# A transformer block on one core: the same 2931 operations in another written-out sequence

## The chip, the cores and the metric

The kernel runs on one core of one Trainium2 chip. The metric is the device time of one execution in microseconds. A core has five engines, each with a queue of its own that it works through in order: TensorE (PE, with the weight loads shown apart as PEld), VectorE (DVE), ScalarE (ACT), GpSimd (POOL) and SyncE (SP). SyncE issues the transfers (DMA) of this kernel. Engines wait for each other by semaphores.

## The reference

One transformer block on x of 2048 rows and 640 columns, in float32:

```python
x = A_x
h = x + _A_ref(_layernorm(x), A_wqkv, A_wo)      # attention
h2 = h + _B_ref(_layernorm(h), w_gate, w_up, w_down)

# _A_ref: 32 heads of 20; row s sees the 8 rows s, s-2, ..., s-14 that exist
logits = einsum("bhsd,bhswd->bhsw", q, kg) * 20 ** -0.5
attn = softmax(where(mask, logits, -1e9))
o = einsum("bhsw,bhswd->bhsd", attn, vg)          # then (o as rows) @ wo

# _B_ref, with 1728 hidden columns
(silu(x @ w_gate) * (x @ w_up)) @ w_down
```

Layernorm has no scale or shift; eps is 1e-5.

## The kernel before, in words

The 2048 rows are taken as four blocks of 512. Every product is done in three passes: each operand is split into a high part (a rounding copy on ScalarE, to fp32r) and a low part (a subtraction on VectorE), and TensorE adds high x high, low x high and high x low. So an operand that is made new costs one instruction on ScalarE and one on VectorE before the matmuls can start, and the matmuls are 512, 384 or 320 columns wide.

The stages, which overlap:

- Start: rows of x come in, are normed, transposed on TensorE (L627) and split (copy L629, subtraction L630). Then the q, k and v projections (L671), four column groups for each block. Results leave PSUM by ScalarE (L680 and others) and go to scratch in DRAM (L701 is a store of k or v rows).
- Attention: for each of 16 pairs of block and group, SyncE loads q (L724) and k and v windows (L728) back. VectorE multiplies q with k (L738, 2560 elements a partition), sums (L745), does the parts of the softmax (L756, L757, L767 to L769), multiplies with v (L773) and adds halves (L780, with 1280 or 640 elements). GpSimd adds some halves (L799). Stores of the attention's output are L813 and L816.
- Output projection: loads L919, splits L923 (ScalarE) and L924 (VectorE), matmuls L943 of 320 columns (L942 in the profile). Layernorm of h follows, with transposes L521, copies L523 and subtractions L513 and L524.
- FFN of blocks 0 and 1: 14 tiles of 128 hidden columns. A tile's weights are loaded (L993; or L999 where the split weights are read back from a store in DRAM), split (copies L994, L995; subtractions L1011), then come three gate passes into PSUM bank 5 and three up passes into bank 6 (five matmuls each, L1017), SiLU (L1040, ScalarE), the multiply by bank 6 (L1041, VectorE), the split of the result (L1051, L1052) and the down product (L1028), which is cut in five pieces of three matmuls into banks 0 to 4. The next tile's up passes need bank 6 back, so they wait for L1041.
- FFN of blocks 2 and 3 together: some tiles as above (L1123; for the last, narrow one L1044 to L1047), then the rest as paired products with fewer multiplications (L1101), whose sums are added on VectorE (L1278) out of banks 5 to 7 and whose operand combinations are made by L1259, L1260 and L1262. Last the down products (L1353, with L1344 and L1345 for their operands) and the final sums and stores (L1164, L1169, L1383).

What sets the order of the work: every operation is handed to `Plan.add` with its engine and what it reads and writes; it gets the next number (0 to 2930) and a set of operations it must come after. `Plan.order` then emits all operations by the tuple `ORDER`, holding an operation back only while one that it depends on is not out:

```python
place = {n: i for i, n in enumerate(ORDER)}
heap, out = [(place.get(n, n), n) for n in range(len(left)) if not left[n]], []
...
    n = heapq.heappop(heap)[1]
    out.append(n)
```

`ORDER` already satisfies the dependences, so it is emitted as it stands, and each engine's queue is the subsequence of its operations. The costs and priorities that `add` is given play no part. An operation is often several instructions (a pass of five matmuls, a piece of downs of three). Operation numbers that the steps below use, in the profiled execution of before: 59, 64, 67 transposes of the start (67 at 16.56 us); 143 to 147, 162 to 164 single matmuls of the first projection; 220 a store of v rows (L701), 264 the load of normed rows (L537), 519 and 521 a q and a k load; 268, 270, 272, 274 low parts of block 1's columns (L546) and 523 the attention product L738 at 56.01; 1396 to 1417, 1590 to 1610, 1710 to 1730 and 1768 to 1788 passes L1017 in the FFN (up passes 1417, 1608, 1728 and 1788 at 364.80, 411.06, 481.45 and 516.53); 848 the shorter L780, 1579 a low part L1052, 1495 an L1429 addition, 1592 the multiply L1041 at 410.33; 1555 a wo product; 868 the v load at 451.83, 1700 the weight load L993 at 450.82, 1664 the L999 load at 449.15, 1505, 1508 and 1511 loads L919, 1635 to 1639 the pieces of downs that end the use of 1664's slot; 1857 to 1860 pieces of downs of two matmuls, 1930 to 1932 products L1101 near 566.

Of the kernel before, what the change touches and what calls it, by code (L numbers as in the profile page):

```python
# [37 lines left out]
    10, 0, 2, 9, 36, 6, 11, 47, 1, 7, 3, 13, 12, 14, 18, 17, 8, 37, 38, 41, 39, 42, 133, 19, 44, 45, 134, 15, 43,  # L38
    135, 136, 16, 48, 21, 52, 22, 46, 40, 26, 49, 20, 23, 137, 138, 53, 54, 139, 25, 27, 140, 141, 24, 30, 50, 51,
    29, 31, 32, 142, 34, 62, 150, 151, 152, 153, 154, 155, 156, 157, 158, 159, 28, 83, 160, 161, 162, 163, 164, 72,  # L40
    33, 55, 79, 78, 82, 86, 64, 80, 87, 81, 94, 90, 65, 59, 60, 70, 66, 71, 67, 68, 69, 91, 63, 95, 143, 103, 102,
    144, 73, 145, 74, 98, 99, 106, 107, 184, 146, 248, 84, 56, 85, 76, 57, 61, 58, 88, 89, 147, 92, 111, 93, 96, 185,
    186, 187, 188, 189, 190, 165, 35, 97, 4, 149, 121, 114, 191, 75, 115, 192, 193, 166, 194, 195, 77, 196, 100, 197,
    198, 101, 104, 108, 105, 167, 168, 169, 170, 148, 5, 199, 171, 172, 173, 174, 118, 175, 176, 177, 178, 179, 180,
    181, 182, 202, 183, 203, 109, 249, 251, 130, 124, 253, 255, 259, 204, 116, 205, 208, 200, 122, 110, 117, 127,
    112, 214, 215, 509, 131, 206, 210, 113, 507, 209, 511, 254, 128, 119, 129, 512, 508, 211, 213, 125, 221, 212,
    230, 120, 252, 201, 216, 513, 222, 263, 207, 224, 250, 262, 123, 260, 232, 223, 256, 226, 257, 261, 219, 218,
    227, 126, 264, 521, 269, 519, 265, 132, 239, 225, 514, 515, 271, 516, 267, 270, 258, 229, 517, 273, 231, 237,
    220, 240, 266, 523, 275, 228, 518, 510, 238, 241, 242, 522, 268, 274, 272, 217, 276, 278, 279, 233, 243, 236,
    1012, 327, 235, 244, 324, 280, 525, 318, 282, 234, 321, 524, 247, 334, 323, 551, 320, 326, 283, 526, 527, 528,  # L50
    529, 520, 325, 530, 531, 246, 245, 322, 340, 553, 328, 286, 343, 281, 289, 290, 287, 319, 532, 533, 288, 337,
    331, 277, 284, 534, 535, 546, 547, 555, 548, 336, 329, 350, 291, 549, 550, 536, 556, 557, 344, 540, 1003, 294,
    335, 541, 552, 538, 342, 558, 539, 559, 545, 298, 330, 300, 345, 353, 296, 292, 560, 301, 332, 537, 333, 339,
    561, 285, 562, 544, 341, 542, 338, 302, 359, 355, 297, 356, 554, 351, 360, 293, 299, 361, 543, 352, 354, 349,
    295, 347, 377, 368, 357, 370, 348, 303, 305, 358, 307, 369, 583, 383, 372, 309, 371, 386, 563, 363, 585, 346,
    1015, 385, 564, 565, 566, 584, 567, 578, 573, 576, 577, 568, 569, 579, 570, 572, 580, 571, 313, 581, 587, 582,
    589, 590, 588, 591, 592, 593, 594, 575, 595, 596, 574, 597, 306, 310, 315, 304, 1006, 379, 314, 364, 308, 317,
    316, 373, 366, 365, 367, 376, 393, 362, 375, 615, 384, 380, 378, 311, 598, 599, 610, 611, 374, 396, 398, 425,
    402, 397, 428, 430, 415, 617, 382, 381, 586, 388, 432, 1009, 395, 434, 399, 387, 312, 394, 390, 392, 391, 612,
    600, 601, 613, 614, 605, 608, 619, 621, 426, 620, 604, 431, 647, 409, 603, 389, 411, 400, 622, 1028, 401, 412,  # L60
    403, 618, 602, 418, 414, 413, 416, 433, 435, 407, 417, 616, 429, 623, 607, 410, 427, 404, 419, 406, 408, 436,
    437, 606, 609, 1035, 422, 439, 420, 421, 445, 442, 405, 441, 1016, 452, 444, 443, 1004, 624, 625, 626, 627, 628,
    630, 461, 446, 447, 631, 633, 634, 635, 636, 637, 642, 643, 644, 645, 646, 649, 651, 653, 652, 654, 1010, 629,
    655, 656, 657, 648, 1013, 632, 438, 455, 1019, 440, 458, 424, 454, 423, 456, 678, 468, 457, 1005, 658, 450, 448,
    453, 638, 639, 1017, 449, 641, 640, 460, 1014, 459, 650, 470, 472, 451, 463, 462, 1020, 659, 464, 469, 482, 1021,
    1007, 660, 661, 662, 1025, 1022, 1023, 467, 663, 1026, 1011, 474, 466, 1024, 1027, 1008, 1029, 1030, 680, 674,
    675, 664, 1031, 1032, 676, 679, 682, 465, 683, 1052, 677, 684, 475, 665, 668, 1033, 1053, 1158, 484, 1036, 1037,
    666, 473, 1038, 1054, 479, 471, 478, 1039, 667, 1034, 1040, 1041, 1042, 485, 1061, 685, 1055, 1058, 1059, 1069,
    709, 1056, 686, 669, 687, 688, 1060, 1062, 480, 1043, 1065, 1057, 1070, 1044, 1045, 488, 501, 477, 689, 1100,
    1160, 476, 483, 1063, 1066, 481, 671, 690, 1159, 673, 672, 670, 711, 1046, 1071, 1064, 1073, 1074, 1067, 1068,  # L70
    691, 1163, 1050, 1047, 692, 1072, 1075, 1048, 693, 694, 1162, 489, 1076, 1077, 705, 499, 500, 497, 495, 486,
    1078, 487, 1049, 1161, 681, 1079, 1080, 1051, 1089, 1176, 1085, 1094, 713, 492, 1097, 1098, 1087, 498, 714, 502,
    1099, 1083, 1084, 1095, 1091, 1081, 1092, 1177, 1086, 1166, 496, 1096, 493, 1082, 1169, 1199, 710, 1088, 1093,
    1090, 1167, 490, 1168, 1164, 706, 707, 695, 503, 1179, 505, 1165, 1170, 504, 1171, 708, 1172, 1184, 715, 506,
    494, 1018, 697, 1201, 698, 716, 1200, 1185, 717, 1180, 1186, 700, 702, 1173, 1187, 1188, 718, 1182, 699, 1178,
    701, 1189, 1204, 703, 1202, 1181, 1190, 1174, 1203, 1207, 1175, 1198, 1208, 696, 712, 1191, 1197, 1210, 719,
    1209, 1192, 1193, 704, 1222, 1211, 1212, 1245, 720, 721, 722, 740, 1223, 1195, 1194, 1217, 1225, 1183, 1213,
    1230, 1214, 1206, 1233, 1196, 1226, 1228, 1215, 1219, 1221, 723, 724, 1246, 1220, 1224, 1216, 1231, 1232, 1205,
    1234, 742, 1227, 1268, 741, 1235, 736, 737, 738, 1249, 1248, 1251, 725, 726, 730, 1218, 727, 1240, 1236, 739,
    746, 1253, 729, 1237, 1241, 1243, 1256, 1247, 747, 1269, 1250, 1254, 1255, 1229, 744, 1110, 745, 743, 1271, 1257,  # L80
    1272, 1291, 1258, 1259, 1276, 748, 1244, 1260, 772, 1279, 1292, 1261, 1274, 749, 1242, 1270, 1238, 750, 1273,
    1239, 728, 1277, 1278, 1314, 751, 752, 1280, 753, 757, 755, 1281, 1264, 1295, 754, 1262, 1294, 1252, 1263, 1282,
    1299, 1300, 756, 1301, 1283, 1302, 731, 735, 1315, 1266, 1297, 733, 734, 1287, 1267, 1303, 1290, 758, 759, 760,
    1318, 1304, 1284, 1265, 1288, 1285, 1305, 1322, 1101, 1311, 1317, 1104, 1306, 1105, 1307, 1107, 761, 732, 1106,
    762, 1108, 1102, 1293, 1323, 1109, 774, 1103, 1324, 1296, 1286, 767, 1111, 1325, 1112, 1326, 768, 776, 1289,
    1309, 1337, 1328, 765, 1338, 1327, 1113, 1316, 769, 1114, 1115, 763, 1117, 766, 764, 775, 777, 1124, 1130, 803,
    1313, 770, 1341, 1345, 771, 1118, 1125, 1319, 1320, 1329, 1312, 1119, 1310, 778, 779, 1120, 1121, 780, 1340, 781,
    1339, 1127, 1275, 1122, 1298, 1308, 1348, 1332, 1126, 1349, 1350, 782, 1133, 1128, 1129, 1330, 1131, 1321, 1342,
    1132, 1346, 1331, 1360, 783, 784, 785, 1134, 1135, 1136, 1123, 786, 1347, 1351, 773, 787, 788, 1383, 805, 1334,
    1137, 1138, 1140, 1361, 1343, 1333, 1356, 1364, 1335, 1363, 1336, 1366, 1352, 789, 1362, 1365, 1367, 1406, 1139,  # L90
    1384, 1368, 799, 800, 1357, 1141, 801, 1142, 1369, 1116, 1371, 1370, 1374, 1143, 802, 791, 807, 1387, 806, 1386,
    1372, 1373, 1144, 1391, 1392, 1393, 1353, 1354, 794, 795, 1375, 1394, 1407, 1145, 1359, 1358, 1381, 1146, 1147,
    808, 1410, 1395, 796, 1376, 793, 1355, 1378, 809, 1397, 834, 1389, 1414, 1409, 1412, 1415, 792, 797, 1148, 1344,
    1149, 1150, 1396, 1382, 1379, 810, 798, 811, 1447, 1385, 1151, 1377, 812, 1405, 813, 1388, 1152, 1401, 1153,
    1398, 790, 814, 1416, 1420, 1429, 1156, 1430, 1157, 804, 1154, 1155, 1417, 1418, 1419, 1380, 1408, 815, 836, 816,
# [1481 lines left out]
```

## Time and profile before

| | |
|---|---|
| median of 3 runs | 836.1 us (834.64 to 836.66) |
| profiled execution | 836.91 us, span 834.6 us |
| granted TensorE clock, mean | 1.0 |
| busy: PE / PEld / DVE / ACT / POOL | 823.7 / 709.1 / 744.3 / 434.9 / 26.3 us |
| DMA | 211.09 MB, mean 253 GB/s |

Busy times are those of the span. L12 is line 12 of the kernel before; the code below the tuple has the same line numbers in both kernels. In a row of the time line the first number is the start in us, the second the length (several instructions of one kind run together have their count behind x), and the bracket at the end is the idle time just before and what released the instruction. Matmuls are pipelined and shown with modelled ends, so the distance of starts says more than the length of one.

### The profile page before, as it was taken

How to read it: one execution, taken by the hardware profiler on the slowest of the kernel's cores; microseconds unless marked ns; L12 is line 12 of the kernel's file. 1: busy time of each engine (PE TensorE's matmuls, PEld its weight loads, DVE VectorE, ACT ScalarE, POOL GpSimd, SP SyncE). 2: the span in 40 equal slices, each digit the busy share in tenths (PEclk: the TensorE clock that was granted, in tenths of full speed). 3: DMA queues.
4: the chain of work that ended last, by engine and by line, in shares of the span. 5: the costliest groups of instructions: out<-in, count | busy, mean ns of one | idle time of the engine just before them, and what ended most of it. 6: DMA issues, size and time to landing. Idle time of an engine off the chain costs nothing.

```text
span 834.6 us, 11331 instructions
## 1 busy us (share of the span) xinstructions
PE 823.7 (99%) x4061; PEld 709.1 (85%) x4061; DVE 744.3 (89%) x906; ACT 434.9 (52%) x824; POOL 26.3 (3%) x34
## 2 busy tenths in 40 slices
PE   8999999999999999999999999999999999999998
PEld 6898898889988889878788888888988888888998
DVE  7589999999999999999999899997759877886984
ACT  7966565243973435845444484664776422233440
POOL 0000000001101000001000000000000000000000
PEclk9999999999999999999999999999999999999999
DMA  8997887756988776689989968899998734357833
GB/s 243 280 343 230 261 248 269 213 177 207 282 301 332 257 240 216 237 254 337 336 276 345 325 201 268 295 276 318 332 323 316 253 131 143 111 176 230 299 127 111
DMA packets 123257, 211.09 MB, mean 253 GB/s; under 512 B 48497, under 2 KB 80945, under 8 KB 122561
## 3 DMA queue, kind: packets, MB, share of 16 engines
q1 hardware_dynamic: 122896, 209.96, 75.7%
q8 instruction: 32, 0.52, 0.3%
q10 hardware_dynamic: 304, 0.41, 0.2%
q14 instruction: 25, 0.20, 0.1%
HBM read 151.27 MB, written 59.05 MB: 252 GB/s over the span
## 4 chain that ended last, share of the span: by engine, by line
PE 71%; DVE 18%; DMA 6%; issue 2%; SPq 1%; ACT 1%; POOL 0%; DVEq 0%; POOLq 0%; ACTq 0%
PE bank L1101 18%; PE bank L671 17%; PE bank L1017 14%; PE bank L1353 7%; PE bank L1028 6%; PE bank L942 4%; DVE fa L773 3%; DVE fa L738 3%; DVE fa L745 3%; DVE fa L780 2%; DMA fa<-vsc 2%; PE bank L1123 2%; PE bank L1158 1%; DMA osc<-fa 1%; DVE ra L1011 1%
## 5 line engine op out<-in xcount | busy, mean ns | idle before, releaser
L1017 PE MATMUL bank<-shb,ra 128*128 128x512 f32 x810 | 194.9, 391 | 3.1 <-DVE fa L1041 2.2
L1017 PEld LDWEIGHTS bank<-shb,ra 128*128 128x128 f32 x810 | 150.9, 188 | 36.8 <-DVE fa L1041 3.1
L671 PE MATMUL bank<-ra,sha 128*128 128x512 f32 (+1 forms) x480 | 105.0, 377 | 1.0 <-ACT sha L629 1.0
L671 PE MATMUL bank<-ra,shb 128*128 128x512 f32 (+1 forms) x470 | 102.3, 377 | 0.0
L671 PEld LDWEIGHTS bank<-ra,sha 128*128 128x128 f32 x480 | 88.2, 188 | 15.7 <-ACT sha L629 1.8
L671 PEld LDWEIGHTS bank<-ra,shb 128*128 128x128 f32 x470 | 86.7, 188 | 14.1
L773 DVE TENSOR_TENSOR fa<-fa 128x2560 f32<-128x2560 f32 x32 | 90.3, 2821 | 3.1 <-DMA fa<-vsc 2.4
L738 DVE TENSOR_TENSOR fa<-fa 128x2560 f32<-128x2560 f32 x32 | 90.2, 2819 | 2.5 <-DMA fa<-qsc 2.1
L745 DVE TENSOR_REDUCE fa<-fa 128x128 f32<-128x2560 f32 x32 | 90.0, 2812 | 0.4
L1101 PE MATMUL bank<-shb,ra 128*128 128x512 f32 x360 | 89.1, 392 | 0.8 <-DMA ra<-lsc 0.8
L1028 PE MATMUL bank<-ra,acts 128*128 128x512 f32 x328 | 84.2, 390 | 0.0
L1101 PEld LDWEIGHTS bank<-shb,ra 128*128 128x128 f32 x360 | 66.5, 188 | 14.5 <-DMA ra<-lsc 1.2
L780 DVE TENSOR_TENSOR fa<-fa 128x1280 f32<-128x1280 f32 (+2 forms) x70 | 76.7, 1096 | 1.5
L942 PE MATMUL bank<-ra 128*128 128x320 f32 x480 | 73.5, 309 | 0.0
L942 PEld LDWEIGHTS bank<-ra 128*128 128x128 f32 x480 | 71.9, 188 | 1.5
L1028 PEld LDWEIGHTS bank<-ra,acts 128*128 128x128 f32 x328 | 61.2, 188 | 12.6 <-DVE h L1429 0.3
L1101 PE MATMUL bank<-ra 128*128 128x512 f32 x288 | 69.9, 391 | 0.0
L1101 PEld LDWEIGHTS bank<-ra 128*128 128x128 f32 x288 | 53.6, 188 | 12.1 <-DVE fa L1278 0.6
L1278 DVE TENSOR_TENSOR fa<-bank,fa 128x512 f32<-128x512 f32 x60 | 40.9, 688 | 20.1 <-PE bank L1101 19.1
L994 ACT CAST ra<-fa 128x1280 fp32r<-128x1280 f32 (+1 forms) x38 | 45.9, 1207 | 17.4 <-DMA fa<-in_ffn_dram 16.8
L1260 ACT CAST ra<-fa 128x512 fp32r<-128x512 f32 x30 | 18.0, 618 | 57.3 <-PE bank L1101 28.7
L1040 ACT ACTIVATE fa<-bank 128x512 f32<-128x512 f32 x34 | 20.3, 598 | 47.8 <-PE bank L1017 40.0
(195 smaller groups left out, 1102.4 us busy)
## 6 DMA issues: line engine op xcount, KB each, us to landing
fa<-in_ffn_dram SPq DMA_DIRECT2D x28, 960.0 KB, 6.8
fa<-ksc SPq DMA_DIRECT2D x16, 880.0 KB, 5.8
fa<-vsc SPq DMA_DIRECT2D x16, 880.0 KB, 6.7
ra<-lsc SPq DMA_DIRECT2D x21, 640.0 KB, 6.3
ra<-lsc SPq DMA_DIRECT2D x27, 320.0 KB, 4.7
lsc<-ra SPq DMA_DIRECT2D x13, 640.0 KB, 3.8
fa<-in_ffn_dram SPq DMA_DIRECT2D x12, 640.0 KB, 5.1
ra<-tsc SPq DMA_DIRECT2D x8, 960.0 KB, 7.6
```

What stands on the lines that cost most here:

```text
L671: T.matmul(banks[bk][:, 0:wide], l, r_(wq(g, w, c), wide), start=(p, c) == first_mm, stop=(p, c) == last_mm)
L738: P.add("DVE", dve(2560), lambda: V.tensor_tensor(f(PROD, 2560).rearrange("p (j w c) -> p j w c", j=2, w=W), window(ko, 2 * jp), f(qo + 32 ...
L745: P.add("DVE", dve(2560), lambda: V.tensor_reduce(f(lo + 128 * jp, 128).rearrange("p (j h w) -> p j w h", j=2, h=8), f(PROD, 2560).rearran ...
L773: V.tensor_tensor(f(PROD, 2560).rearrange("p (w n d) -> p n w d", w=W, d=DH), bass.AP(tensor=fa[:, vo : vo + 160].tensor, offset=fa[:, vo ...
L780: V.tensor_add(f(dst, 320 * m), f(PROD, 320 * m), f(PROD + 320 * m, 320 * m))
L942: T.matmul(banks[bk][:, 0:320], l, r_(m, 320), start=not seeded and p == 0 and c == 0, stop=p == 2 and c == NC - 1, skip_group_check=seeded)
L994: P.add("ACT", act(n), lambda: A.copy(r_(gu, n), f(raw, n)), r=[rf(raw, n)], w=[rr(gu, n)], prio=PR["fh"])
L1017: T.matmul(banks[bk], r_(gu + 1280 * w + wid * c + col, 128), x2(a, c), start=p == 0 and c == 0, stop=p == 2 and c == NC - 1)
L1028: T.matmul(banks[bk][:, lo:hi], l, m, start=first and p == 0, stop=last and p == len(passes) - 1)
L1101: T.matmul(banks[bk], r_(ws[w] + 256 * q, 128), x(a, c), start=start and p == n == q == 0, stop=stop and p == 2 and n == len(terms) - 1 an ...
L1278: dv(0, lambda: V.tensor_add(fb(h, dst), banks[bk], fb(h, src)), [pb(bk)] + fr(h, src), fr(h, dst))
L1353: T.matmul(banks[bks[j]][:, 0:320], t(a, 128, 128 * j), r_(ws[w], 320), start=p == q == 0, stop=p == NP - 1 and q == 2)
```

## The change

Only the tuple `ORDER` is replaced. It holds the same 2931 numbers; 2834 of its places hold another one. The code, the operations and what each depends on are the same; each engine's queue is a permutation of what it was:

| engine | planned operations | at another place in the queue | largest shift in places |
|---|---|---|---|
| TensorE | 808 | 513 | 23 |
| ScalarE | 647 | 526 | 31 |
| VectorE | 845 | 617 | 113 |
| SyncE | 613 | 510 | 58 |
| GpSimd | 18 | 0 | 0 |

The new sequence too satisfies all dependences as it stands. The diff is 153 lines of numbers for 153; two pairs of them (around operations 264 and 1608):

```diff
 ORDER = (
...
-    227, 126, 264, 521, 269, 519, 265, 132, 239, 225, 514, 515, 271, 516, 267, 270, 258, 229, 517, 273, 231, 237,
...
-    1592, 1605, 1498, 1495, 1606, 1593, 1608, 1500, 1603, 1609, 1490, 1502, 1599, 1610, 1607, 1598, 1620, 1494, 1492,
...
+    256, 213, 230, 222, 218, 512, 250, 220, 131, 257, 128, 129, 119, 120, 264, 513, 122, 224, 226, 123, 216, 126,
...
+    1590, 1578, 1605, 1592, 1593, 1608, 1494, 1498, 1491, 1594, 867, 1609, 1623, 1621, 1606, 1604, 1502, 1500, 1610,
...
```

What it makes of single queues, at the places that the prediction speaks of (consecutive operations of that engine):

```
TensorE  before  162 163 164 64 59 67 143 144 145 184 146 56
         after   143 144 145 162 64 146 59 163 67 56 164 147
SyncE    before  262 260 261 219 218 264 521 519 220 275
         after   261 262 219 218 220 264 521 519 275
VectorE  before  514 515 516 270 258 517 266 523 268 274
         after   514 515 516 258 517 268 266 272 274 523 525 270
TensorE  before  1396 1382 1379 1405 1401 1416 1417
         after   1396 1414 1381 1402 1380 1415 1378 1416 1417
TensorE  before  1590 1605 1606 1608 1609
         after   1590 1605 1608 1609 1606
VectorE  before  1577 1579 845 846 847 848 1592 1498 1495
         after   1495 1489 842 843 844 1577 845 846 847 1592 1498 1594
SyncE    before  899 897 1511 1505 888 1504 1664 1508 1700 891 868
         after   899 1664 1505 1508 1511 1504 868 888 1700 891
TensorE  before  1710 1726 1718 1727 1728
         after   1710 1697 1725 1726 1727 1719 1717 1716 1728
TensorE  before  1770 1758 1775 1788 1555
         after   1770 1757 1785 1786 1777 1787 1779 1755 1555 1758 1788
TensorE  before  1884 1860 1857 1897 1898 1899 1930 1931 1932
         after   1884 1858 1857 1897 1859 1860 1898 1899 1930 1931 1932
```

290 rows, old and new, of the table ORDER are left out of this document.

## The prediction

> **What bounds the kernel now.** The first look is at the page: the busy shares, then the chain that ended last by engine.
>
> ```profile
> PE 823.7 (99%) x4061; PEld 709.1 (85%) x4061; DVE 744.3 (89%) x906; ACT 434.9 (52%) x824; POOL 26.3 (3%) x34
> PE 71%; DVE 18%; DMA 6%; issue 2%; SPq 1%; ACT 1%; POOL 0%; DVEq 0%; POOLq 0%; ACTq 0%
> ```
>
> TensorE is busy 823.7 of 834.6 us, so all its idle time is 10.9 us, and no order of the same 4061 matmuls can win more than that. The second look is at what TensorE waited for; columns are microseconds in total, times, longest.
>
> ```profile
> PE bank L1017 <- DVE fa L1041: 2.2, 4, 0.9
> PE bank L571 <- POOL ra L1456: 1.3, 1, 1.3
> PE bank L671 <- ACT sha L629: 1.0, 2, 0.7
> PE bank L1101 <- DMA ra<-lsc: 0.8, 1, 0.8
> PE bank L627 <- ACT sha L629: 0.7, 1, 0.7
> PE bank L1017 <- ACT shb L523: 0.7, 1, 0.7
> ```
>
> These sum to 6.7 us. The largest kind is the up projection (L1017) that waits for the gate multiply (L1041) on VectorE to free bank 6. The third look is at stretches of the span, to see who else is full (columns: length, busy of PE, PEld, DVE, ACT, POOL, granted clock, DMA share, GB/s).
>
> ```profile
> 60.00:236.00 176.00, 175.83 (x867) 153.97 (x866) 173.66 (x152) 99.54 (x234) 9.96 (x10) 1.00 0.77 241
> 236.00:411.00 175.00, 173.26 (x800) 144.74 (x800) 170.04 (x178) 90.45 (x143) 7.23 (x8) 1.00 0.80 275
> 411.00:562.00 151.00, 149.72 (x704) 125.88 (x704) 145.03 (x147) 82.81 (x134) 7.81 (x8) 1.00 0.86 286
> 562.00:650.00 88.00, 87.22 (x479) 77.25 (x478) 66.47 (x121) 58.78 (x101) 0.00 (x0) 1.00 0.92 317
> 650.00:766.00 116.00, 116.00 (x523) 95.81 (x522) 92.98 (x147) 34.67 (x66) 0.10 (x1) 1.00 0.49 164
> ```
>
> Up to 562 us VectorE is almost as full as TensorE (173.66 of 176, then 170.04 of 175), because the attention runs there. After that it has room. So up to 562 a wait of TensorE for VectorE goes only as far as VectorE itself comes earlier; that decides what each removed wait is worth.
>
> **The change part by part.** Nothing is added or removed: the same operations, in other places of each engine's queue. So the terms are waits that go and waits that come. A removed wait is costed as the start after it less the end of the work before it, at the spacing of 512-column matmuls. The rows of TensorE (start, busy, line, count, idle and releaser in brackets):
>
> ```profile
> 16.56 0.33 PE L627 MATMUL bank<-fa 128*128 128x128 f32 x1 [0.73 <-ACT sha L629]
> 333.09 2.91 PE L1028 MATMUL bank<-ra,acts 128*128 128x512 f32 x12
> 336.09 1.43 PE L1017 MATMUL bank<-shb,ra 128*128 128x512 f32 x5
> 363.33 1.29 PE L1017 MATMUL bank<-shb,ra 128*128 128x512 f32 x5
> 364.80 1.43 PE L1017 MATMUL bank<-shb,ra 128*128 128x512 f32 x5 [0.17 <-DVE fa L1041]
> 407.80 2.43 PE L1017 MATMUL bank<-shb,ra 128*128 128x512 f32 x10
> 411.06 1.65 PE L1017 MATMUL bank<-shb,ra 128*128 128x512 f32 x6 [0.84 <-DVE fa L1041]
> 479.87 1.29 PE L1017 MATMUL bank<-shb,ra 128*128 128x512 f32 x5
> 481.45 1.43 PE L1017 MATMUL bank<-shb,ra 128*128 128x512 f32 x5 [0.29 <-DVE fa L1041]
> 509.78 4.47 PE L1017 MATMUL bank<-shb,ra 128*128 128x512 f32 x19
> 514.09 0.84 PE L1028 MATMUL bank<-ra,acts 128*128 128x512 f32 x3
> 516.53 1.39 PE L1017 MATMUL bank<-shb,ra 128*128 128x512 f32 x5 [0.92 <-DVE fa L1041]
> 564.75 1.07 PE L1101 MATMUL bank<-shb,ra 128*128 128x512 f32 x4
> 566.59 1.65 PE L1101 MATMUL bank<-shb,ra 128*128 128x512 f32 x6 [0.78 <-DMA ra<-lsc]
> ```
>
> Spacing: (514.09 - 509.78)/19 = 0.227 us. A wait is then, for example at 481.45, 481.45 - (479.87 + 5 x 0.227) = 0.45. The others in the same way: 336.09 gives 0.28, 364.80 gives 0.34, 411.06 gives 0.99 (ten matmuls from 407.80), 516.53 gives 1.08 (six from 514.09: the three of this row and three with the operands swapped), 566.59 gives 0.93.
>
> [...]
>
> *Up to 411.* Here stands the one gate wait that the new order does not cover. Before, two up passes of ten matmuls in all lie between the last use of bank 6 and the next; after, one gate pass (operation 1605, five matmuls), with operation 1606 put behind operations 1608 and 1609. What VectorE has ahead of the multiply:
>
> ```profile
> 403.74 0.69 DVE L1052 TENSOR_TENSOR acts<-fa,acts 128x512 fp32r<-128x512 f32 x1 [0.69 <-ACT acts L1051]
> ...
> 408.06 2.35 DVE L780 TENSOR_TENSOR fa<-fa 128x1280 f32<-128x1280 f32 x2
> 410.33 0.68 DVE L1041 TENSOR_TENSOR fa<-bank,fa 128x512 f32<-128x512 f32 x1
> 410.93 1.28 DVE L1429 TENSOR_TENSOR h<-bank,h 128x512 f32<-128x512 f32 x2
> ```
>
> The subtraction at 403.74 and the shorter L780 of the pair move behind the multiply, one L1429 (1.28/2 = 0.64) comes ahead: -0.69 - 0.83 + 0.64, about -0.85 in all. The 0.69 us in which VectorE waited ahead of 403.74 goes too. The multiply then ends at 411.01 - 0.85 - 0.69 = 409.5. TensorE reaches the up pass at 407.80 + 5 x 0.227 = 408.9 or sooner, so it still waits; after it come the five matmuls of operation 1606, so 409.5 + 1.1 = 410.6 compares with 411.06 of before: a gain of 0.4. All that TensorE wins earlier is swallowed here: the transposes at 16.56 (four qkv products from behind are put before them: -0.7), the late cast at 336.09 (-0.3), the gate wait at 364.80 (seven operations, 27 matmuls or 6.1 us, in place of 17 matmuls or 3.9 us: -0.3), and also the new waits before it (at 246 and 394 an operation has 0.6 to 0.8 us more queued ahead than its slack). More is won only if VectorE is earlier at that point. Its one larger gap before is this:
>
> ```profile
> 53.27 0.68 DVE L546 TENSOR_TENSOR shb<-fa,shb 128x512 fp32r<-128x512 f32 x1
> 56.01 2.83 DVE L738 TENSOR_TENSOR fa<-fa 128x2560 f32<-128x2560 f32 x1 [2.06 <-DMA fa<-qsc]
> ```
>
> Three more subtractions that are ready go ahead of it and one goes behind (L546, some 0.6 each beside the next), which fills up to 1.2, but a store of V rows (operation 220) goes ahead of the q load in SyncE's queue and may cost as much, so 0 to 1.2. The part takes -1.0, the middle of -0.4 and -1.6.
>
> *411 to 562.* At 481.45 four pieces of downs and three passes, 27 matmuls or 6.1 us, stand between the uses of bank 6, where 13 (2.9 us) did. At 516.53 three gate passes, five pieces of downs and a wo product (L942, fifteen narrower matmuls) come in front where six matmuls did. Both waits go: -0.45 - 1.08. VectorE must keep up for that, and there its one large gap is the wait for V values:
>
> ```profile
> 463.23 2.83 DVE L773 TENSOR_TENSOR fa<-fa 128x2560 f32<-128x2560 f32 x1 [2.40 <-DMA fa<-vsc]
> ```
>
> ```profile
> 444.75 0.81 SPq L919 DMA_DIRECT2D fa<-osc  x2
> 449.15 0.32 SPq L999 DMA_DIRECT2D ra<-lsc  x1
> 451.83 0.53 SPq L728 DMA_DIRECT2D fa<-vsc  x1
> ```
>
> ```profile
> fa<-in_ffn_dram SPq DMA_DIRECT2D x28, 960.0 KB, 6.8
> ```
>
> The second fence is SyncE's queue (start of the issue, its length, line), the third the size of the weight loads L993. The V load at 451.83 (operation 868) goes ahead of one such weight load and of two small stores. At 286 GB/s of this stretch 960 KB are 3.4 us, more than the gap of 2.40, so VectorE gains up to 2.4 there, which covers the attention steps that are now nearer to the gate multiplies. Against it, three wo loads (L919) go behind a weight load (L999, operation 1664) that waits for its slot; in the trace that load is issued at 449.15, when the last piece of downs has freed the slot, but those pieces also stand some 10 us of TensorE work earlier, so I cost it at nothing. With that cover gone (the pieces no earlier) the wo loads come 449.15 - 444.75 = 4.4 later; a wo product that now stands ahead covers 2.1 of it, and 2.3 reach TensorE.
>
> *566.59.* The weights (L999) that came late are issued when their slot in the weight store comes free. Two more pieces of downs (0.45 each) go before the product that needs them and two small loads behind: -0.9.
>
> *New waits.* The order is also tighter elsewhere. Counting what is put ahead of each releasing operation against the slack that it had, deficits of 1.0 to 1.6 come out at 550 to 561 (the gate of the last tile, L1045 and L1047, two pieces of attention and of columns ahead of it) and of 1.0 to 1.5 at 624 to 634, and in the pair stage up to 1.8. VectorE waits for TensorE in most of those places:
>
> ```profile
> DVE fa L1278 <- PE bank L1101: 19.1, 24, 1.5
> 697.76 0.69 DVE L1278 TENSOR_TENSOR fa<-bank,fa 128x512 f32<-128x512 f32 x1 [0.96 <-PE bank L1101]
> ```
>
> so a deficit there is mostly paid from that idle time (at 697.76 the deficit is 1.8, the idle time just before 0.96). The bounds are 0 and 4.0, all three places in full (1.6 + 1.5 + 0.9 that is left at 697.76); I take +1.5, nearer to nothing because the rows show waiting VectorE. SP, ACT and POOL: POOL's sequence is the same, ACT is at 52%. The last sums and stores after 766 change places only among themselves: nothing.
>
> Sum: -1.0 - 0.45 - 1.08 - 0.93 + 1.5 = -2.0. The profiled execution took 836.91 us in all (span 834.6 and 2.3 around it), 0.8 above the median of 836.1. So 834.9 by its own measure, and 836.1 - 2.0 = **834.1** as a median.
>
> **The rivals.** *The waits only move* (836.2): VectorE gains nothing at 56 and 463, so 0.4 at 411 and 2.46 behind are followed by new waits of 1.6 at 550 to 561 and about 1.4 after: 0.4 + 2.46 - 3.0 = about nothing. For it: VectorE at 170.04 of 175. Against it: the V load really goes ahead of 960 KB.
>
> *All waits go* (831.4): TensorE is idle 0.17 + 1.74 + 1.28 + 0.78 = 3.97 us by the stretches (60 to 650); without them and the 0.73 at 16.56, -4.7 and 836.1 - 4.7. For it: the cover at 481 and 516 is far more than needed. Against it: 411 stays bound.
>
> *The pair stage turns into the bound* (839.1, slower). TensorE is busy 116.00 of 116.00 us there, so any wait counts in full. The additions of products (L1278) free the banks; in the new order other VectorE work (L1262, L1164) goes ahead of several of them. Six of the deficits (0.9 to 2.5 us each, at 693 to 771) sum to 8.5 if none eases the next, and the largest alone is 2.5; the middle, 5.5, in place of the 0.5 that the new waits have for that stage gives -2.0 + 5.0 = +3.0. It decides from about 2.5 us of idle TensorE between 650 and 831 on, where the sum turns to zero. Against it: VectorE waits 19.1 us for TensorE there.
>
> **How the numbers follow.** What a measurement of this kernel can tell from no change is about 0.3%, 2.5 us: faster is below 833.6, slower above 838.6. Chances: forecast 0.40 (own range 832.9 to 835.4), moved waits 0.22, all waits gone 0.24, pair stage 0.14. A third of the forecast's own range lies below 833.6, so faster is 0.24 + 0.14 = 0.38; slower 0.14; within 0.3% the rest, 0.48. The range is 831.0 to 838.3: it holds the forecast and the moved waits, most of the case with all waits gone, and the lower edge of the pair stage.
>
> **What would show it.** Right: no wait of L1017 for L1041 near 481 and 516, one of 0.5 to 2 us at about 409; no wait of L1101 for lsc; the V wait of VectorE shorter than 1 us; the L999 load near 447 issued at about 440 and L919 loads not behind 449. Wrong: a wait of VectorE for fa<-qsc above 3 us near 56; TensorE below 115 of 116 us in the pair stage; more than 2 us of new waits between 545 and 640; total idle of TensorE (10.9 now) not between 7 and 11.

## The result and the profile after

| | before | after |
|---|---|---|
| median | 836.38 us (4 runs) | 831.13 us (4 runs, 830.67 to 831.80) |
| ratio, 95% interval | | 0.9942 [0.9924, 0.9959] |
| profiled execution, span | 836.91, 834.6 us | 831.80, 829.5 us |

So the new sequence is 5.25 us faster, where 2.0 were forecast. The measured 831.13 lies outside the forecast's own range (832.9 to 835.4) and within 0.3 us of the rival in which all waits go (831.4). One execution of e5 below had a granted clock of 0.758 and took 1016.67 us; it is left out of the times. The page after, busy shares and the chain that ended last:

```profile
PE 821.0 (99%) x4061; PEld 709.1 (85%) x4061; DVE 742.1 (89%) x906; ACT 437.3 (53%) x826; POOL 26.2 (3%) x34
PE 95%; DVE 3%; DMA 1%; ACT 0%; SPq 0%; issue 0%; DVEq 0%; ACTq 0%
```

The second line says most: VectorE's share of the chain went from 18% to 3% and TensorE's from 71% to 95%. Idle time of TensorE is 829.5 - 821.0 = 8.5 us. That is only 2.4 less than before, while the span is 5.1 shorter; the other 2.7 is in the busy time (823.7 to 821.0), which holds part of each wait (at 411.06 before, the bracket has 0.84 and the starts give 0.99). So the 10.9 us of idle time are not the bound on what an order can win that the prediction took them for. What TensorE waited for:

```profile
PE bank L671 <- ACT ra L645: 2.5, 1, 2.5
PE bank L571 <- POOL ra L1456: 1.3, 1, 1.3
PE bank L1017 <- DVE fa L1041: 0.4, 1, 0.4
PE bank L1017 <- ACT shb L512: 0.2, 1, 0.2
```

One gate wait of four is left, and no wait for lsc. The 2.5 us at the start are new. The same stretches as before:

```profile
60.00:236.00 176.00, 175.76 (x866) 153.88 (x865) 172.87 (x154) 100.09 (x234) 10.41 (x10) 1.00 0.76 239
236.00:411.00 175.00, 174.60 (x811) 146.93 (x810) 170.61 (x178) 90.54 (x143) 7.37 (x8) 1.00 0.83 282
411.00:562.00 151.00, 151.00 (x711) 126.95 (x710) 145.55 (x146) 86.61 (x139) 7.19 (x8) 1.00 0.87 289
562.00:650.00 88.00, 87.95 (x483) 78.34 (x483) 67.40 (x121) 59.90 (x103) 0.00 (x0) 1.00 0.90 320
650.00:766.00 116.00, 116.00 (x535) 96.85 (x534) 94.50 (x152) 34.72 (x66) 0.10 (x1) 1.00 0.52 170
```

From 411 to 650 TensorE is idle 0.05 us, where it was idle 1.28 + 0.78. The places themselves, in TensorE's rows:

```profile
9.31 0.51 PE L671 MATMUL bank<-ra,sha 128*128 128x512 f32 x1 [2.50 <-ACT ra L645]
...
235.69 2.56 PE L1017 MATMUL bank<-shb,ra 128*128 128x512 f32 x10 [0.24 <-ACT shb L512]
...
361.62 4.47 PE L1017 MATMUL bank<-shb,ra 128*128 128x512 f32 x19
...
404.69 2.20 PE L1017 MATMUL bank<-shb,ra 128*128 128x512 f32 x9
407.29 3.02 PE L1017 MATMUL bank<-shb,ra 128*128 128x512 f32 x12 [0.40 <-DVE fa L1041]
...
477.78 1.98 PE L1028 MATMUL bank<-ra,acts 128*128 128x512 f32 x8
479.59 2.66 PE L1017 MATMUL bank<-shb,ra 128*128 128x512 f32 x11
...
517.00 0.86 PE L1028 MATMUL bank<-ra,acts 128*128 128x512 f32 x3
517.70 2.44 PE L1017 MATMUL bank<-shb,ra 128*128 128x512 f32 x10
...
560.48 3.69 PE L1101 MATMUL bank<-shb,ra 128*128 128x512 f32 x14
```

The up passes 1417, 1728 and 1788 now stand at 362.5 (inside the row at 361.62), 479.59 and 517.70 with no bracket, and the products at 560.48 too. Only 1608, at 407.29, still waits: 407.29 - (404.69 + 9 x 0.227) = 0.56.

**Where the time went, from several profiles.** One profile per kernel turned out not to be enough to answer this, since what is lost at loads and at the start differs between executions (near 566 by 0.67 to 3.61 us, at the start by 6.75 to 7.41, in the table). Each experiment below left a profile too, most with whole stretches in one of the two sequences. So I took for each profile the lost time of TensorE: the start of a matmul less the spacings of all matmuls before it (0.2265 us for 512 columns, 0.1735 for 384, 0.147 for 320, 0.109 for transposes, 814.5 us in all). The table gives what is lost between two points, counted in microseconds of TensorE's work so that the same work is compared; a profile is used where its stretch is wholly one sequence and not edited.

| work of TensorE, us | old sequence, mean (range, profiles) | new sequence | difference |
|---|---|---|---|
| 0 to 24: start | 7.12 (6.75-7.41, 7) | 5.91 (5.24-6.47, 5) | -1.20 |
| 24 to 300: projections, 236 | 2.26 (1.61-2.83, 6) | 1.29 (1.28-1.31, 4) | -0.97 |
| 300 to 390: 336, 364, 373 | 1.40 (1.38-1.44, 6) | 0.33 (0.33-0.33, 3) | -1.08 |
| 390 to 410: the wait at 411 | 1.37 (1.35-1.42, 7) | 0.70 (0.70-0.71, 2) | -0.67 |
| 410 to 545: 481, 516 | 0.70 (0.42-2.08, 6) | 0.68 (0.53-0.98, 4) | -0.02 |
| 545 to 580: 566 | 1.39 (0.67-3.61, 8) | 0.66 (0.65-0.68, 5) | -0.73 |
| 580 to 814 | 1.46 (1.39-1.55, 8) | 0.88 (0.80-0.94, 5) | -0.58 |

The sum is -5.25, the measured difference. Three quarters of it, 3.9 us, lie ahead of the end of the gate wait at 411.

### The profile page after: what moved, and what is told of

The parts are those of the page before. It is cut to its first block, busy times and chain, and to the rows that moved or that the text cites. A ratio compares the mean times of both kernels' runs of the same rounds, so it can differ in the third digit from the quotient of the medians.

```text
span 829.5 us, 11354 instructions
## 1 busy us (share of the span) xinstructions
PE 821.0 (99%) x4061; PEld 709.1 (85%) x4061; DVE 742.1 (89%) x906; ACT 437.3 (53%) x826; POOL 26.2 (3%) x34
## 4 chain that ended last, share of the span: by engine, by line
PE 95%; DVE 3%; DMA 1%; ACT 0%; SPq 0%; issue 0%; DVEq 0%; ACTq 0%
PE bank L671 25%; PE bank L1017 20%; PE bank L1101 18%; PE bank L1028 10%; PE bank L942 8%; PE bank L1353 7%; PE bank L1123 2%; PE bank L1158 1%; PE bank L1148 1%; DMA fa<-in_wqkv_dram 1%; DMA ra<-lsc 1%; DVE shb L546 0%; DVE fa L773 0%; DVE fa L738 0%; DVE fa L745 0%; PE bank L521 0%
## 5 line engine op out<-in xcount | busy, mean ns | idle before, releaser
L1017 PE MATMUL bank<-shb,ra 128*128 128x512 f32 x810 | 193.9, 390 | 0.6 <-DVE fa L1041 0.4
L1017 PEld LDWEIGHTS bank<-shb,ra 128*128 128x128 f32 x810 | 151.5, 188 | 32.4 <-DVE fa L1041 0.8
L745 DVE TENSOR_REDUCE fa<-fa 128x128 f32<-128x2560 f32 x32 | 90.0, 2812 | 0.4
L942 PE MATMUL bank<-ra 128*128 128x320 f32 x480 | 73.8, 309 | 0.0
L942 PEld LDWEIGHTS bank<-ra 128*128 128x128 f32 x480 | 71.9, 188 | 1.9 <-ACT bank L935 0.3
L680 ACT ACTIVATE st<-bank,fa 128x480 f32<-128x480 f32 x48 | 30.9, 662 | 28.3 <-PE bank L671 28.3
```

Source lines behind the costliest of these rows:

```text
L745: P.add("DVE", dve(2560), lambda: V.tensor_reduce(f(lo + 128 * jp, 128).rearrange("p (j h w) -> p j w h", j=2, h=8), f(PROD, 2560).rearran ...
L942: T.matmul(banks[bk][:, 0:320], l, r_(m, 320), start=not seeded and p == 0 and c == 0, stop=p == 2 and c == NC - 1, skip_group_check=seeded)
L1017: T.matmul(banks[bk], r_(gu + 1280 * w + wid * c + col, 128), x2(a, c), start=p == 0 and c == 0, stop=p == 2 and c == NC - 1)
```

## The experiments

All kernels hold the same operations, and only the sequence is edited, so that each queue not named is as it was. In e1 to e4 the tuple is one line shorter, so L1016 there is L1017 elsewhere. A diff shows consecutive operations of one queue. The old sequence's median beside them was 836.52 (e1 to e4), 836.75 (e5 to e8) and 836.54 us (e9 to e12).

**e1, the wait at 516 alone** (TensorE's queue).

```diff
- 1775 1788 1555 1785 1786 1787 1779
+ 1775 1555 1785 1786 1787 1788 1779
```

> The kernel before with one move in TensorE's queue alone: the up pass at 516.53 (operation 1788) goes behind the wo product and the three gate passes that followed it. Theory A, a covered wait is worth its own length at the end: the wait of L1017 for L1041 near 516 goes, 1.2 us with the slow second start, and the time falls by 1.2 us. Theory B, VectorE sets the pace up to 562: the wait goes at its place but comes back as new waits between 545 and 566, and the end moves by less than 0.4 us.

836.51 us, ratio 1.0002 [0.9993, 1.0011]: nothing. Its waits of L1017 for the multiply:

```profile
PE bank L1016 <- DVE fa L1040: 1.0, 2, 0.9
```

These are the one at 411 (0.9) and a trifle near 365. The wait at 516 is gone, but it is gone in six other profiles of that stretch as well (e2 to e4 and e9 to e11), where nothing was done there: the largest loss between 500 and 510 us of work is 0.15. So neither theory is tested; the wait was one of the execution that was profiled before, not of the kernel.

**e2, the waits at 364 and 373 alone** (TensorE's queue).

```diff
- 1401 1416 1417 1418 1419 1380 1402 1437 1438 1439 1440 1403
+ 1401 1416 1380 1402 1417 1418 1419 1437 1438 1439 1403 1440
```

> The kernel before with moves in TensorE's queue alone: two pieces of downs go ahead of the up pass at 364.80 (operation 1417) and one ahead of that at 373.33 (operation 1440), so that both gate waits, 0.45 and 0.34 us, go. Theory A: 0.8 us less at the end, and the wait at 411 stays at 1.1. Theory B, the step of the prediction that the gate wait at 411 swallows what TensorE wins ahead of it: the wait at 411 grows by 0.8 to 1.9 us and the end moves by less than 0.3 us.

836.14 us, ratio 0.9994 [0.9985, 1.0003]: -0.4, not told from nothing. TensorE near 411, then VectorE:

```profile
408.23 2.65 PE L1016 MATMUL bank<-shb,ra 128*128 128x512 f32 x11
412.43 1.89 PE L1016 MATMUL bank<-shb,ra 128*128 128x512 f32 x7 [1.54 <-DVE fa L1040]
```

```profile
405.10 0.69 DVE L1051 TENSOR_TENSOR acts<-fa,acts 128x512 fp32r<-128x512 f32 x1 [0.69 <-ACT acts L1050]
...
411.69 0.68 DVE L1040 TENSOR_TENSOR fa<-bank,fa 128x512 f32<-128x512 f32 x1
```

The two waits are gone, and the wait at 411 is 412.43 - (408.23 + 11 x 0.227) = 1.70 in place of 1.0: what was won 40 us earlier is given back, as theory B says. VectorE works the same queue at the same pace up to this multiply, its own 0.69 of waiting included. The 0.23 us that it waits for TensorE at 378 in the other profiles are gone here, but its next wait, for GpSimd's addition at 380, is 1.00 us in place of 0.68, so nothing of the win reaches the multiply.

**e3, the multiply at 411 alone** (VectorE's queue).

```diff
- 846 847 848 1592 1498
+ 846 1592 847 848 1498
```

> The kernel before with one move in VectorE's queue alone: the multiply at 410.33 (operation 1592) goes ahead of the two L780 additions of 2.35 us. Theory A: the wait at 411 (1.1 us) goes and the time falls by 1.1 us. Theory B: the wait goes, but as VectorE itself is no earlier the waits at 481 and 516 grow from 0.6 and 1.2 by about 1 us, and the end moves by less than 0.4 us.

836.46 us, ratio 1.0001 [0.9992, 1.0010]. The wait at 411 is gone, but 3 us later stands another:

```profile
408.15 5.38 PE L1016 MATMUL bank<-shb,ra 128*128 128x512 f32 x23
414.50 0.96 PE L1027 MATMUL bank<-ra,acts 128*128 128x512 f32 x3 [0.97 <-DVE h L1428]
```

A piece of downs waits for its bank, which an addition of VectorE (L1429) empties. Neither theory had this place, but B's kind is right: VectorE is as late as before, and TensorE meets it at the next bank.

**e4, the V load alone** (SyncE's queue).

```diff
- 1508 1700 891 868
+ 1508 868 1700 891
```

> The kernel before with one move in SyncE's queue alone: the load of V values that VectorE waits 2.40 us for at 463 (operation 868) goes ahead of the 960-KB weight load and of the small store that stood before it. Both theories: the wait of VectorE at 463 falls below 0.5 us. Theory B, VectorE sets the pace: the multiplies at 481 and 516 come some 2 us earlier, both gate waits (0.6 and 1.2) go with TensorE's order as it was, and the time falls by 1.5 to 1.8 us. Theory A, only cover in TensorE's queue counts and VectorE's earliness is taken up by its own order: the waits stay above 0.3 and 0.8 and the time falls by less than 0.5 us.

836.30 us, ratio 0.9999 [0.9990, 1.0008]. VectorE has no wait at 463 and the gate waits at 481 and 516 are gone, but they are also gone in e2 and e3, where VectorE waits at 463 for 0 and 0.42 us. The 2.40 of the profile before is the longest of all; e1 has 0.57. In this execution the weights came late near 566 instead:

```profile
PE bank L1100 <- DMA ra<-lsc: 3.2, 1, 3.2
```

By starts of matmuls the wait for these weights is 0.7 to 3.4 us in five profiles of the old sequence there (the one before, e2, e4, e9, e11), and e1, e3 and e10 do not list it. The single profile of before had made typical of the kernel what changes between its executions.

**e5 and e6, the two halves.** One sequence up to TensorE's operation that started at 425 us before, then what is left, in the other's relative order.

```diff
- ORDER = old
+ ORDER = new[:k] + [n for n in old if n not in new[:k]]      (e5)
+ ORDER = old[:k] + [n for n in new if n not in old[:k]]      (e6)
```

> The new sequence up to TensorE's operation that started at about 425 us, and all that is left in the old relative order. The one profile of each kernel puts the lost time of TensorE at that point at 11.6 us before and 8.8 after; the profiles of the three single moves put the old order's at 11.7 to 13.0. Theory A, gains add up by place: 2.8 to 3.5 us of the 5.3 come, 832.9 to 833.6. Theory B, VectorE's lead is what counts and later waits go with it: 4.3 us or more, 832.1 or less.

> The counterpart: the old sequence up to 425 us, and what is left in the new relative order. Theory A: the rest of the gain, 1.8 to 2.5 us, 833.9 to 834.6. Theory B: VectorE has no lead to hand on, so 0.9 us or less, 835.5 or more.

e5: 831.68 us, ratio 0.9934 [0.9913, 0.9955], -5.1. e6: 836.13 us, ratio 0.9989 [0.9975, 1.0003], -0.6, not told from nothing. (Of e5 only the times are used.) Both went as B expected, in time. Most is won ahead of 425. The split by the table above, some 3.9 there and 1.3 behind, lies inside both intervals too.

**e7, the V load late again in the new sequence** (SyncE's queue).

```diff
- 1504 868 888 1700 891 890
+ 1504 888 1700 891 868 890
```

> The changed kernel with one move in SyncE's queue alone: the load of V values (operation 868) goes back behind the 960-KB weight load and the two small stores. The prediction's step that VectorE must keep up, by way of this load: VectorE waits 1 to 2.4 us there, a gate wait comes back between 475 and 562, and the time rises by 0.8 to 2.4 us. Against it: the new order's cover at 481 and 516 (6.1 and 9.0 us for lags of 3.3 and 2.3) takes it up, and the time rises by less than 0.4.

830.94 us, ratio to before 0.9924 [0.9906, 0.9942], as good as the changed kernel. VectorE shows no wait of over 0.15 us for V values even so. The prediction's point that this load carries the stretch falls.

**e8, two more moves in the new sequence** (TensorE's and SyncE's queues).

```diff
- 1605 1608 1609 1606        - 18 16 17 21
+ 1605 1606 1608 1609        + 18 17 16 21
```

> The changed kernel with two moves: gate pass 1606 goes back ahead of up pass 1608 (TensorE), where the changed kernel still waits 0.67 us at 407, and the second weight load of the start (L642, operation 17) goes back ahead of a load of x (SyncE), where TensorE waits 2.5 us for the cast of these weights. If each wait is worth its length, about 0.7 and 1.0 (the matmuls after it then wait for VectorE's low parts), so 829.4; if VectorE sets the pace after both, less than 0.4 comes, 830.7 or more.

831.89 us, ratio to before 0.9934 [0.9913, 0.9954]: no gain beside e7, which was measured with it. The wait at 407 is gone (0.04 in place of 0.70 lost between 390 and 410) and nothing came back behind. But the start lost 7.8 us instead of 5.9: TensorE still waited for the second weights' cast, and then ran slowly.

```profile
8.66 0.49 PE L671 MATMUL bank<-ra,sha 128*128 128x512 f32 x1 [1.22 <-ACT ra L645]
...
10.80 4.53 PE L671 MATMUL bank<-ra,sha 128*128 128x512 f32 x13
```

Thirteen matmuls take 13 x 0.227 = 2.95 us elsewhere; here 4.53. The granted clock (the third number from the end) was 0.55 from 10 to 12 and 0.60 from 12 to 14 us:

```profile
10.00:12.00 2.00, 2.00 (x9) 1.72 (x8) 1.43 (x4) 1.56 (x4) 0.00 (x0) 0.55 0.96 326
12.00:14.00 2.00, 2.00 (x6) 1.56 (x6) 2.00 (x5) 1.94 (x5) 0.00 (x0) 0.60 0.99 333
```

In the changed kernel and in e12 it is 1.00 in both stretches. So e8 does not tell what its move at the start is worth. The move at 407 is in e12 too.

**e9 and e10, where in the first half.** As e5, with the cut at 228 and at 300 us.

> The new sequence up to TensorE's operation that started at about 228 us (start and projections), then the old relative order, with the old gate waits at 364, 373 and 411. Theory A, gains by place: only what the start brings, 1.0 to 1.4 us by the profiles so far, 835.3. Theory B, VectorE's lead: VectorE gets the start's gain too, and the L924 subtraction that takes 1.79 us in every profile of the old order (0.42 in the new) is short, so its multiplies come 2.4 us earlier, the waits at 364, 373 and 411 (1.9 us) go as well, and 2.5 to 3.3 us come: 833.3 to 834.1.

> The new sequence up to about 300 us, then the old one, so TensorE gains the start and the place near 236, 2.3 us ahead of the old gate waits. The prediction's step that the wait at 411 swallows what TensorE wins ahead of it: the wait at 411 is 2 us or more and the time falls by 1.3 us at most. Theory A: 2.3 us, 834.3. Theory B, VectorE has the same lead and the gate waits go too: 3.3 us or more, 833.3 or less.

e9: 834.03 us, ratio 0.9978 [0.9967, 0.9989], -2.5. e10: 833.15 us, ratio 0.9967 [0.9955, 0.9978], -3.4. With e5 this makes a staircase: -2.5 up to 228, -3.4 up to 300, -5.1 up to 425. In time both came out in or next to B's numbers, but not for B's reason: in e9 the waits at 364, 373 and 411 did not go (0.31, 0.21 and 1.00 by starts; 0.34, 0.23 and 1.00 before), and in e10 only the first two did, where its seam had made TensorE later. The list of waits shows one for L1041 in e9, of 0.8, and in e10 this, with the one wait that is new there:

```profile
PE bank L942 <- ACT bank L935: 1.2, 1, 1.2
PE bank L1017 <- DVE fa L1041: 0.8, 1, 0.8
```

By starts of matmuls the wait at 411 is 1.00 in e9 and 0.99 in e10, as it is in the old sequence (1.00 to 1.02), although TensorE has lost 1.3 and 1.2 us less by then than the mean of the old sequence (10.8 at 395 us of work). So what was won ahead of 300, in e10 less what its seam cost (the L942 wait at 319, 1.3 by starts), went through the gate wait whole; the step of the prediction that e10 was to test is refuted. VectorE had come along. Its multiplies before, and then in e9:

```profile
243.86 0.69 DVE L1041 TENSOR_TENSOR fa<-bank,fa 128x512 f32<-128x512 f32 x1 [0.43 <-PE bank L1017]
298.98 0.69 DVE L1041 TENSOR_TENSOR fa<-bank,fa 128x512 f32<-128x512 f32 x1 [0.43 <-PE bank L1017]
```

```profile
298.14 0.69 DVE L1041 TENSOR_TENSOR fa<-bank,fa 128x512 f32<-128x512 f32 x1 [0.47 <-PE bank L1017]
...
409.47 0.68 DVE L1041 TENSOR_TENSOR fa<-bank,fa 128x512 f32<-128x512 f32 x1
```

VectorE waits for TensorE at these places, so it starts again when TensorE lets it: 0.84 us earlier at 298 and 0.86 at 410 (410.33 before), where TensorE has lost 0.85 less at 395 us of work (9.43, and 10.28 before). In e10 the multiply at 410 is 0.68 earlier and 0.67 less is lost. Both profiled executions were 1.0 and 1.2 us above their medians, so by the profiles alone e9 would have won the 1.2 us of the start. The wait for weights near 566, 1.47 us by starts in e9's profile and absent in some others, can make up such an excess; where the other 1.3 of e9's median come from is not shown.

**e11, VectorE without GpSimd in its way** (VectorE's queue).

```diff
- 662 1011 1024                - 787 1364 1363 1352 789 1365 799
+ 1011 662 1024                + 787 799 1364 1363 1352 789 1365
```

> The kernel before with two moves in VectorE's queue alone: the low part of wo (L829, operation 1011) goes ahead of the product L738 near 190, and the sum L745 (operation 799) goes directly behind the product L738 near 333, ahead of the subtractions L1011. The two subtractions that took 1.79 and 1.84 us beside GpSimd's addition L799 (instead of 0.42 and 0.82) are expected at 0.42 and 0.82 us. Theory B: VectorE is 2.4 us earlier, the waits at 364, 373 and 411 shrink by 1.5 us or more together, and the time falls by 1.2 to 2.4 us. Theory A: TensorE's queue is unchanged, so less than 0.4 us comes.

835.36 us, ratio 0.9993 [0.9982, 1.0005]: not told from nothing. The waits at 364 and 373 went (0.6 us), the one at 411 stayed at 0.99. The second collision was avoided, the first was not, since another subtraction (L829) came to stand beside GpSimd's addition and took 2.19 us in place of 0.82; its rows stand in the last section. So the test of a VectorE that is 2.4 us earlier was not had: of 2.4 us only 1.0 came, and at 348 VectorE waited 0.68 us for ScalarE, which no other profile of the old sequence shows. Ahead of 300 us of work this profile also lost more than the others (3.15, in place of 1.61 to 2.83).

**e12, three moves at the new sequence's own waits** (TensorE's as in e8, ScalarE's and VectorE's).

```diff
- 1095 498 1087 1085 1089 1092 1083 1081 1177      - 1352 1365 794 799
+ 1095 1087 1085 1089 1092 1083 1081 498 1177      + 1352 799 1365 794
```

> The changed kernel with three moves at its own remaining waits: gate pass 1606 back ahead of up pass 1608 (wait of 0.67 us at 407), the eviction of a projection (L690, operation 498, 0.74 us of ScalarE) behind the column copies that TensorE waits 0.5 us for near 235, and the sum L745 (operation 799) ahead of the subtraction L1011 (operation 1365) that takes 1.60 us beside GpSimd's addition. If each wait is worth its length now that VectorE has a lead: 1.2 us less, 829.9. If the waits come back behind: less than 0.4, 830.7 or more.

830.28 us, ratio to before 0.9928 [0.9916, 0.9940]. Its waits of TensorE are those of the start alone:

```profile
PE bank L571 <- POOL ra L1456: 1.3, 1, 1.3
PE bank L671 <- ACT ra L645: 1.2, 1, 1.2
```

Behind the start it loses 3.2 us in its profile, the changed kernel 4.4 and 4.5 (e7): the expected 1.2 are there and stay to the end. In the medians it is 0.85 below the changed kernel, but the two intervals overlap, so that it beats the changed kernel is likely and not shown. It is faster than the kernel before beyond doubt.

## Why the prediction was right, and where it was not

The direction and the range were right and the size was not: -2.0 against -5.25. By its own steps:

- **Up to 411, -1.0 forecast, -3.9 found.** The step that failed is "All that TensorE wins earlier is swallowed here". What the prediction said behind it, "More is won only if VectorE is earlier at that point", held: VectorE was earlier, because ahead of that point it waits for TensorE itself. In the old sequence it does so near 244 in all seven profiles that have it there (0.42 to 0.51 us) and near 299 in seven of eight (0.43 to 0.47), in the new one near 250:

```profile
249.69 0.69 DVE L1041 TENSOR_TENSOR fa<-bank,fa 128x512 f32<-128x512 f32 x1 [1.73 <-PE bank L1017]
```

  At such a place a win of TensorE reached VectorE (in e9 the multiply at 298 came 0.84 us earlier). So -1.2 from the start and -1.0 near 236 passed (e9 and e10, with the wait at 411 unchanged). Whether VectorE would have kept up without its shorter subtraction near 193 (0.41 or 0.42 us in place of 1.79, also in e9 and e10) is open, since e11 did not get that test. A win behind 299 was swallowed in e2, to the tenth: 0.7 won, 0.7 given back. The new sequence kept the 1.1 of 336, 364 and 373, and there VectorE's queue is moved too (the multiply for 364 stands ahead of the 2.8-us transposition L529 that it stood behind); which of the moves does it was not tested. The multiply ends at 407.2, where 409.5 was worked out:

```profile
406.55 0.68 DVE L1041 TENSOR_TENSOR fa<-bank,fa 128x512 f32<-128x512 f32 x1
...
407.92 0.69 DVE L1052 TENSOR_TENSOR acts<-fa,acts 128x512 fp32r<-128x512 f32 x1
```

  The L1052 behind it and the waiting that went with it are as forecast; the start was not in the sum, nor were 1.6 us that the subtractions near 193 and 337 took less (1.79 and 1.84 before, 0.42 and 1.60 after). The place near 236 (the 0.7 for L523 in the prediction's list of waits) was not costed. Four transposes L521 that stood behind the last projection (at 235.35) stand ahead of it in the new sequence, and the wait behind it falls from 0.84 to 0.40 us by starts.
- **411 to 562, -1.5 forecast, 0.0 found.** The two waits were measured rightly in a profile that had them by chance: six other profiles of the old sequence (e4's, with the V load moved, among them) lose 0.40 to 0.43 us from 410 to 545 where that one lost 2.08. The V load's early place, which was to earn it, is worth nothing (e4, e7). It was issued early, as forecast, and so was the L999 load, ahead of the wo loads and 10.4 us earlier than before (449.15):

```profile
438.75 0.54 SPq L999 DMA_DIRECT2D ra<-lsc  x1
439.34 3.74 SPq L919 DMA_DIRECT2D fa<-osc  x3
...
443.77 0.60 SPq L728 DMA_DIRECT2D fa<-vsc  x1
```

- **566, -0.9 forecast, -0.7 found.** Right. In the old sequence this wait spreads most (0.67 to 3.61 lost from 545 to 580), in the new one it is 0.65 to 0.68 in five profiles. That is likely also why the new sequence's times spread less (830.7 to 831.8); this was not tested by itself.
- **New waits, +1.5 forecast, none found; -0.6 behind 580 instead.** This term was mis-sized too. Behind the wait at 407 the list of TensorE's waits after has none, and in the pair stage VectorE still waits for TensorE almost as long as before (19.1):

```profile
DVE fa L1278 <- PE bank L1101: 18.8, 23, 2.1
```

  With nothing in place of +1.5 the forecast would have been nearer by 1.5. The -0.6 behind 580 is made of losses under 0.15 us each, and its cause is open.
- **The start.** Only the wait at 16.56 was costed. In fact four waits of the start went (at 6.94, 8.55, 9.83 and 16.56, 1.95 us together by their brackets) and one of 1.2 to 2.5 us, for the cast of the second weights, took their place. That this one was coming was not seen.
- **The rivals.** "All waits go" was right in its number, 831.4, but by other places: nearly a quarter of the gain is the start, and 481 and 516 gave nothing. So that number came out by luck. "The waits only move" is what e2 and e3 did, each a single move. The pair stage did not become the bound: 0.58 us less is lost behind 580.
- **The signs.** Everything that the prediction named as a sign of being right came true: no gate wait near 481 and 516, 0.56 us at 407, no wait for lsc, no V wait of 0.2 us, the L999 load issued at 438.75, the last wo load at 442.62. The same signs would have stood beside a gain of 2 us, so they could not tell the two sizes apart. The errors of the four parts, -2.9, +1.5, +0.2 and -2.1, partly cancel.

## What to carry to other kernels

Before a wait in a profile is costed, see whether it is there in a second profile of the same order: here those that end with a load (and those that follow from one) came and went between executions (the one near 566 was 0.7 to 3.4 us in five profiles and not listed in three), while the gate wait at 411, set by two engines' queues, was 1.00 to 1.02 us in the profiles of the old sequence. Where two engines are both nearly full, ask at which places the second waits for the first. Here a win ahead of such a place went on to the end (e9, e10), and a win behind it was given back at the next bank that both use (e2). That fits why the single moves gave nothing here and whole stretches, with every queue moved, up to 5 us; two of the single moves (e1, e4) were aimed at waits that most executions do not have.

## What the runs showed of the hardware that was not expected

Some subtractions of VectorE took longer beside GpSimd's additions: 1.79 us near 193 before, where the same one takes 0.42 us after. VectorE and GpSimd before, then after:

```profile
192.70 2.39 DVE L924 TENSOR_TENSOR ra<-fa,ra 128x512 fp32r<-128x512 f32 x2
...
192.79 2.02 POOL L799 TENSOR_TENSOR fa<-fa 128x640 f32<-128x640 f32 x1
```

```profile
192.33 1.02 DVE L924 TENSOR_TENSOR ra<-fa,ra 128x512 fp32r<-128x512 f32 x2
...
336.69 1.60 DVE L1011 TENSOR_TENSOR ra<-fa,ra 128x640 fp32r<-128x640 f32 x1
...
192.56 1.58 POOL L797 TENSOR_TENSOR fa<-fa 128x1 f32<-128x1 f32 x1 [55.93 <-DVE fa L738]
...
335.44 2.17 POOL L799 TENSOR_TENSOR fa<-fa 128x640 f32<-128x640 f32 x1
```

The same two subtractions take 2.39 us before and 1.02 after. The second of them takes 1.79 us in all six profiles with the old sequence there and 0.41 or 0.42 in those with the new, so it is the order and not chance. After, it is GpSimd's instruction at 192.56 that takes longer: 1.58 us for one element a partition, where the other eleven L797 of that profile take 0.19 to 0.64. The 1.60 at 336.69 (0.78 in other orders) ends 0.68 us after GpSimd's addition does. In e11:

```profile
194.62 2.19 DVE L829 TENSOR_TENSOR ra<-fa,ra 128x640 fp32r<-128x640 f32 x1
...
336.65 2.82 DVE L745 TENSOR_REDUCE fa<-fa 128x128 f32<-128x2560 f32 x1
339.38 1.55 DVE L1011 TENSOR_TENSOR ra<-fa,ra 128x640 fp32r<-128x640 f32 x2
...
336.90 1.56 POOL L799 TENSOR_TENSOR fa<-fa 128x640 f32<-128x640 f32 x1
```

With the sum L745 beside it, GpSimd's addition takes 1.56 us and the sum 2.82, neither longer than elsewhere (before, ten of the twelve additions take 1.56 to 1.58, and the sums 2.81 in the mean), and the two subtractions that come after take 1.55 together. The subtraction L829 that now starts at 194.62, beside GpSimd's other addition (194.38 to 196.14), takes 2.19 in place of 0.82. Near 264 before it is the other way round: the subtraction L1011 starts at 264.74, GpSimd's addition at 264.83, and the subtraction takes its 0.82 us, the addition 2.15 in place of 1.57. Why the one or the other takes longer is not shown.

The start of e8 is the other point: after a wait of TensorE of 1.22 us (to 8.66), six of the matmuls from 10.80 us on came 0.43 us or more apart instead of 0.227, at the granted clock of 0.55 and 0.60 shown with e8. In the changed kernel a longer wait (2.50, to 9.31) and in e12 one as long (1.2) left the clock at 1.00. So the matmuls of e8 were slow where the clock was lowered, and what lowered it there and not in the other two is not shown.

The diff's 153 lines told of above are the hunk with its context; the tuple has 147 lines of numbers in both kernels.
